# SyncE issues every transfer: the weights, their gradients and the late cache loads move from GpSimd's DMA queue to SyncE's

## The chip, the core and the metric

The kernel runs on one core of a Trainium2 chip. The core has five engines that work side by side, each with an instruction queue of its own: TensorE (PE in the profile, PEld for its weight loads), VectorE (DVE), ScalarE (ACT), GpSimd (POOL) and SyncE (SP). Sixteen DMA engines move data between the chip's memory (HBM) and the core's SBUF; a transfer is issued by an engine's queue and then runs by itself. SyncE computes nothing: it waits and issues. A transfer that SyncE issues and one that GpSimd issues go through different rings of the same sixteen DMA engines; in the profile they are q1 (hardware_dynamic) and q0 (software_dynamic).

The metric is the device time of one execution in microseconds.

## What is computed

The program is the forward and the backward pass of one decode step: a grouped-query attention block over a cache, in parallel with a bilinear gated MLP, both on the same normalised input of 2 rows of 576.

```python
x  = A_x                                  # [2, 1, 576]
xn = layernorm(x)
q = (xn @ wq) -> 32 heads of 128          # wq [576, 4096]
scores = q @ k^T * 128**-0.5              # k_cache, v_cache [2, 16, 4096, 128], 2 query heads to one of the cache
p = softmax(scores);  o = p @ v
A = o @ wo                                # wo [4096, 576]
B = ((xn @ w_gate) * (xn @ w_up)) @ w_down   # [576, 4608] twice, [4608, 576]
out_0 = x + A + B
out_1..out_8 = gradients of x, k_cache, v_cache, wq, wo, w_gate, w_up, w_down for grad_out
```

Everything is bf16. The two caches are 33.6 MB each, and their gradients as large; the five weights are 25.4 MB together, and their gradients as large. So every cache and every weight is read once and a gradient of the same size is written: by the profile 92.48 MB are read and 92.48 MB written.

## The kernel before

**Steps.** The 16 cache heads are taken two at a time (8 groups, `NG`), for each of the 2 batch rows: 16 steps, `s` in the code. A step has four cache tiles of 1 MB (K and V of two heads), each 128 partitions by 4096 elements, 8192 contiguous bytes a partition. For each tile VectorE turns 32x32 blocks (`turn`, L421), TensorE makes scores (L1105) from the turned tile, softmax and its gradient follow, TensorE contracts probabilities and their gradients with the straight tile (L1282), and the gradients of K and V are outer products (L1127) of a [4096] vector with a row of 128. For these GpSimd spreads the row into a block-diagonal tile BD (L1093, 3.6 us each, 32 of them). ScalarE and VectorE bring each product from PSUM to a 1 MB staging tile (`cp`, L425 and L427, four evictions of 128x1024 to a tile), and the tile is stored.

**Weights.** Beside the steps run 8 attention groups (wq and wo slabs of 512 columns or rows, `group_front`, `group_back`) and 9 MLP slabs of 512 (`mlp`). The gradients of the weights are outer products of short vectors as well (`rows_outer`, `cols_outer`, `tail_outer`), staged and stored in the same way. In HBM a slab of 512 columns is strided: each of its rows is a run of 1024 bytes. A 128x4x512 slab has four such runs to a partition; the 576 rows of a weight leave a tail of 64 rows of 512 columns, moved by itself. The wq tail is 128 rows of 512 bytes (L1009), as its two halves go to two halves of the partitions. A 128x4x576 slab has four runs of 1152 bytes a partition; the w_down slab has 4608 contiguous bytes.

**Buffers.** Sixteen 1 MB buffers (`big`) serve three uses with a cap each (`CAP`): straight cache tiles (8), turned tiles (13), staging tiles of stores (5). One buffer pair holds the gate and up slab (`gu`, one slot), five hold the other weight slabs (`ww`).

**Order.** No engine's order is written out by hand. The functions are generators, one for each stream of work; they yield requests (an operation on an engine with its cost, a buffer, an event, a DMA), and a planner (`Order`) runs through them in a made-up time when the program is built: of the requests that can start within a small slack of the earliest, it takes the one with the lowest priority number, and writes the instruction. Priorities are `STEP * s + PR[name]` with amendments for the first two and the last two steps (`HEAD`, `TAIL`). `Lines` is the planner's model of the two DMA rings. What engine evicts a product (ACT or DVE) is also the planner's choice (`EV`). On the chip each engine then runs its list strictly in order: an instruction that waits for a semaphore holds back everything behind it on its engine.

**Who issues.** SyncE issues the cache loads (`load_kv`, L995, in the last two steps GpSimd does), the cache gradients' stores (`put`, L654, with `KVSTORE`), w_down (L1035), and group 0's wq tail. GpSimd issues the wq, wo, gate and up slabs and tails (L1009, L1013, L1018, L1028, L1031) and all weight gradients' stores (`put` again, L654). SyncE has 132 transfers, GpSimd 136. GpSimd also builds BD (L1093) and the score weights W (L1070). ScalarE issues the two loads of x and grad_out. The transfers of a ring use eight completion semaphores in turn, so an issue waits until the one eight before it in that ring has landed.

Of the kernel before, what the change touches and what calls it, by code (L numbers as in the profile page):

```python
# [52 lines left out]
class Lines:  # L53
# [5 lines left out]
    def run(self, until=None):  # L59
        line = self.line  # L60
        while (line[0] or line[1]) and (until is None or self.now < until):
# [21 lines left out]
            for k in live:  # L83
                if line[k][0].work < 1e-9 or k == first:
                    line[k].pop(0).t = self.now + 1.4
# [19 lines left out]
class Order:  # L105
# [3 lines left out]
    def __init__(self):  # L109
# [7 lines left out]
        self.log = []  # L117

# [44 lines left out]
    def start(self, s):  # L163
        r = s.req
# [19 lines left out]
        if r[0] == "dma":  # L184
            return max(s.ready, self.free[r[1]]), r[1]
# [7 lines left out]
    def run(self):  # L193
        while self.streams:
# [37 lines left out]
            elif r[0] == "dma":  # L232
                self.free[e] = t + r[2]
                s.land = self.lines.push(e == "POOL", t + r[2] + LATENCY[e], r[3], r[4])
                s.ready = t + r[2]
                self.log.append((t, r[2], e, s.gen.__name__))
# [51 lines left out]
def DMA(engine, cost, nbytes, row=8192):  # L288
    packet = 0.0375 * row + 9.0
    return ("dma", engine, cost, 0.08 + nbytes / 16e3 * packet / row, packet)  # L290
# [4 lines left out]
CAP = {"kv": 8, "X": 13, "st": 5}  # L295
MLP0, MLPD = 0, 7.51
KVSTORE = "SP"
WQ0, WO0 = 0, 1
LATENCY, DRY = {"SP": 0.5, "ACT": 0.5, "POOL": 0.57}, 0.4
LM = 0.0  # L300
CLK = 2.0
BIAS = 0.52
SLACK = {"PE": 0.07, "ACT": 0.09, "DVE": 0.43, "POOL": 8.93, "SP": 17.19}
STEP = 28.0
HEAD = {"turn0": -27.5, "turn1": 17.9, "att": -70.5, "dsc": 20.0, "con": 10.4, "out1": 26.9, "out0": -42.2, "front": 26.2, "back": -304.6, "W0": 9.7, "W1": 90.3, "BD1": 30.3, "BD0": 91.5}
TAIL = {"turn0": 70.2, "turn1": -109.5, "att": -6.3, "dsc": -1.8, "con": -89.5, "conv": -4.6, "out1": -9.2, "out0": -5.8, "front": 37.9, "back": 9.6, "W1": -49.5, "BD1": 7.5, "BD0": -113.0, "load": -33.0}
PR = {"turn0": -74.6, "turn1": -110.6, "att": -719.4, "dsc": -725.3, "conv": 70.0, "con": -246.1, "out1": 1310.1, "out0": 250.5,
      "front": 190.0, "back": -43.0, "W0": 65.6, "W1": 62.0, "BD1": 442.2, "BD0": -91.5, "mlp": -115.0, "wout": -277.2,
      "store": 413.8, "load": -5.8, "wload": -723.6, "fin": 24.5, "const": 23.5, "mload": -44.2}


def pr(name, s):
    edge = {} if type(s) is not int else HEAD if s < 2 else TAIL if s > 13 else {}
    return STEP * s + PR[name] + edge.get(name, 0)
# [3 lines left out]
def kernel(  # L318
# [331 lines left out]
    def put(engine, parts, tag, slot, events=(), row=8192):  # L650
        def run():
            for j, (dst, src, nbytes) in enumerate(parts):
                yield DMA(engine, 0.78 if engine == "POOL" else 0.36, nbytes, row)
                (nc.gpsimd if engine == "POOL" else nc.sync).dma_start(dst, src)  # L654
# [40 lines left out]
    def rows_outer(lhs, dst, p, events=()):  # L695
# [3 lines left out]
        store = Store(FC, put("POOL", [(dst, src, 128 * FC * D * 2)], "st", i, events, 4608), p)  # L699
# [3 lines left out]
    def cols_outer(rhs, dst, p, events=()):  # L703
# [3 lines left out]
        store = Store(2, put("POOL", [(dst, src, 128 * 4 * FS * 2)], "st", i, events, 4096), p)  # L707
# [3 lines left out]
    def tail_outer(rhss, dsts, p, events=()):  # L711
# [4 lines left out]
        store = Store(2, put("POOL", parts, "tl", i, events, 4096), p)  # L716
# [20 lines left out]
    def mlp(i, Lgu, Ld, gs_slot, wd_slot):  # L737
# [42 lines left out]
        po = pr("mlp", (MLP0 + i * MLPD) / 4) + PR["wout"]  # L780
# [204 lines left out]
    def load_kv():  # L985
        n = 0
        for s in range(NS):
            g, b = divmod(s, Bq)
            yield PRIO(pr("load", s))
            for t in range(2):  # L990
                for l in range(G):
                    i = yield ACQ("kv")
                    late = s > NS - 3
                    yield DMA("POOL" if late else "SP", 0.78 if late else 0.36, 1 << 20)
                    (nc.gpsimd if late else nc.sync).dma_start(kv_t[i][:], views[t][b, G * g + l])  # L995
# [5 lines left out]
    def load_w(item):  # L1001
        kind, i = item
        if kind in ("wq", "wo"):
# [3 lines left out]
            if kind == "wq":  # L1007
                yield DMA("POOL" if i else "SP", 0.6, 128 * 256 * 2, 4096 if i else 512)
                (nc.gpsimd if i else nc.sync).dma_start(ww_t[w][:, 4 * FS:WB],  # L1009
                                                        A_wq[512:576, n0:n0 + FS].rearrange("p (h n) -> h p n", h=2))  # L1010
                yield ("lset", st["Lq"])
                yield DMA("POOL", 0.78, 128 * 4 * FS * 2, 4096)
                nc.gpsimd.dma_start(ww_t[w][:, 0:4 * FS].rearrange("p (c n) -> p c n", n=FS),  # L1013
# [424 lines left out]
```

## Time and profile before

| | us |
|---|---|
| median of 3 runs | 482.54 (481.98 to 483.42) |
| the profiled execution | 483.63 |
| its span, first to last instruction | 481.8 |
| busy PE / DVE / ACT / POOL | 377.4 / 350.0 / 345.7 / 248.6 |
| DMA: 185.93 MB in 33444 packets | mean 386 GB/s |
| mean granted TensorE clock | 0.651 |

The span is shorter than the execution by what lies before the first and after the last instruction. The page's DMA row gives the busy share of the sixteen DMA engines in 40 slices, the GB/s row what they moved; part 3 splits both by ring. A DMA engine counts as busy from a packet's start to its end, however slowly the packet moves, so a share near one and a low GB/s figure can stand together. The table by stretches gives for each engine the busy time with the number of instructions, then the granted clock, the DMA share and the GB/s. The waits name an instruction, what it waited for, the total, the number of waits and the longest.

### The profile page before, as it was taken

The page shows a single profiled execution, that of the slowest core. Times are in us where ns is not written, and L with a number is a line of the kernel's source. Part 1 is how long each engine was busy: PE and PEld are TensorE (multiplying, and loading weights), DVE is VectorE, ACT ScalarE, POOL GpSimd, SP SyncE. Part 2 cuts the span into 40 slices and gives each one's busy share as a digit, 9 for nine tenths or more (in the row PEclk, how much of TensorE's full clock was granted, in tenths as well). Part 3 has the DMA queues.
Part 4 walks back from the last instruction along what each step waited for, and adds up shares of the span by engine and source line. Part 5 has one row for each costly group of instructions (what it writes and reads, how often), then busy time and mean ns, then how long its engine had stood idle before and what let it go on. Part 6 is the DMA issues. An engine that isn't in the chain of part 4 may idle for free.

```text
span 481.8 us, 14584 instructions
## 1 busy us (share of the span) xinstructions
PE 377.4 (78%) x6122; PEld 213.5 (44%) x6122; DVE 350.0 (73%) x658; ACT 345.7 (72%) x529; POOL 248.6 (52%) x356
## 2 busy tenths in 40 slices
PE   0577977688852889879988997787797887599987
PEld 0444545443521554525553554444452545344544
DVE  6678856786747868677677878687686779398873
ACT  6059975598961688966758974799786973497993
POOL 6176803784146763451557624865715873265502
PEclk9999575666955666655555656667675665655695
DMA  8999999999999989999999999999999999999795
GB/s 298 387 402 327 414 396 422 384 379 388 423 414 373 389 335 333 400 419 398 415 399 409 366 394 422 397 413 421 411 392 421 420 416 395 402 403 375 280 407 198
DMA packets 33444, 185.93 MB, mean 386 GB/s; under 512 B 5034, under 2 KB 5170, under 8 KB 16994
## 3 DMA queue, kind: packets, MB, share of 16 engines
q1 hardware_dynamic: 18714, 131.22, 67.7%
q0 software_dynamic: 14656, 53.77, 29.7%
q8 instruction: 48, 0.79, 0.6%
q14 instruction: 18, 0.15, 0.1%
q10 hardware_dynamic: 8, 0.00, 0.0%
HBM read 92.48 MB, written 92.48 MB: 384 GB/s over the span
## 4 chain that ended last, share of the span: by engine, by line
DMA 37%; PE 29%; ACT 14%; DVE 10%; issue 5%; POOL 4%; SPq 0%; DVEq 0%; ACTq 0%; POOLq 0%
DMA out_dram<-big 23%; ACT big L425 11%; DMA gu<-in_B_w_up_dram 10%; PE ps_o L1127 6%; PE ps_m L1105 5%; PE ps_m L1282 5%; DVE big L421 4%; DMA gu<-in_B_w_gate_dram 3%; DMA big<-in_A_k_cache_dram 2%; POOL BD L1093 2%; DVE big L427 2%; PE ps_m L768 2%; PE ps_o L674 1%; PE ps_m L750 1%; PE ps_m L1193 1%
## 5 line engine op out<-in xcount | busy, mean ns | idle before, releaser
L425 ACT CAST big<-ps_o 128x1024 bf16<-128x1024 f32 (+1 forms) x324 | 288.2, 961 | 41.7 <-PE ps_o L1127 31.3
L421 DVE STREAM_TRANSPOSE big<-big 128x1024 f32<-128x1024 f32 x128 | 152.7, 1218 | 15.3 <-DMA out_dram<-big 10.8
L1093 POOL TENSOR_TENSOR BD<-vr,mask 128x2048 bf16<-128x2048 bf16 x32 | 115.3, 3602 | 31.2 <-ACT vr L425 16.6
L1105 PE MATMUL ps_m<-big,W 128*32 128x128 bf16 x2048 | 60.3, 285 | 9.6 <-POOL W L1070 4.8
L427 DVE CAST big<-ps_o 128x1024 bf16<-128x1024 f32 (+1 forms) x52 | 59.4, 1143 | 9.8 <-PE ps_o L1127 3.6
L1127 PE MATMUL ps_o<-BD,pp 32*128 32x512 bf16 x256 | 54.6, 544 | 14.1 <-ACT big L425 6.7
L1105 PEld LDWEIGHTS <-W 128*32 128x32 bf16 x2048 | 47.8, 127 | 28.4 <-issue 20.2
L654 POOL DMA_DIRECT2D out_dram<-big x43 | 33.4, 777 | 44.1 <-ACT big L425 26.5
L1070 POOL COPY W<-rep 32x16 bf16<-32x16 bf16 x128 | 24.5, 192 | 58.7 <-DVE rep L873 53.8
L1127 PE MATMUL ps_o<-BD,dd 32*128 32x512 bf16 x256 | 49.9, 530 | 6.0 <-ACT big L425 5.3
L421 DVE STREAM_TRANSPOSE big<-ww 128x1152 f32<-128x1152 f32 x25 | 34.0, 1359 | 7.6 <-DMA out_dram<-big 7.2
L1282 PE MATMUL ps_m<-big,pp 128*32 128x512 bf16 x256 | 32.1, 605 | 2.5 <-DVE accx L834 1.5
L1127 PEld LDWEIGHTS <-pp 32*128 32x128 bf16 x256 | 12.0, 99 | 37.3 <-issue 32.6
L625 POOL COPY wt<-wm 64x128 bf16<-64x128 bf16 (+1 forms) x34 | 8.9, 262 | 37.5 <-DVE wm L618 33.3
L1282 PE MATMUL ps_m<-big,dd 128*32 128x512 bf16 x256 | 26.7, 505 | 1.3 <-DVE hb L755 0.8
L421 DVE STREAM_TRANSPOSE big<-gu 128x1024 f32<-128x1024 f32 x18 | 21.8, 1223 | 3.0 <-DMA out_dram<-big 2.2
L1127 PEld LDWEIGHTS <-dd 32*128 32x128 bf16 x256 | 11.0, 99 | 26.6 <-issue 20.5
L654 POOL DMA_DIRECT2D out_dram<-tl x26 | 14.4, 557 | 15.9 <-ACT tl L425 6.6
L632 PE MATMUL ps_m<-big,wm 128*32 128x128 bf16 x416 | 13.8, 293 | 9.1 <-DVE big L421 7.9
L1292 ACT ACTIVATE osb<-ps_m 128x512 bf16<-128x512 f32 x15 | 9.1, 606 | 15.7 <-PE ps_m L1282 15.7
L674 PEld LDWEIGHTS <-xnr 32*128 32x128 bf16 x416 | 15.2, 117 | 8.3 <-issue 6.9
L674 PE MATMUL ps_o<-hb,xnr 32*128 32x128 bf16 x288 | 17.0, 271 | 2.3 <-ACT big L425 0.7
(210 smaller groups left out, 561.4 us busy)
## 6 DMA issues: line engine op xcount, KB each, us to landing
out_dram<-big SPq DMA_DIRECT2D x64, 1024.0 KB, 11.3
big<-in_A_k_cache_dram SPq DMA_DIRECT2D x28, 1024.0 KB, 12.7
big<-in_A_v_cache_dram SPq DMA_DIRECT2D x28, 1024.0 KB, 17.2
out_dram<-big POOLq DMA_DIRECT2D x26, 512.0 KB, 11.7
out_dram<-big POOLq DMA_DIRECT2D x17, 576.0 KB, 9.5
ww<-in_B_w_down_dram SPq DMA_DIRECT2D x9, 576.0 KB, 15.0
ww<-in_A_wo_dram POOLq DMA_DIRECT2D x8, 576.0 KB, 14.3
gu<-in_B_w_gate_dram POOLq DMA_DIRECT2D x9, 512.0 KB, 13.0
```

The lines of the kernel that those rows point to most:

```text
L421: nc.vector.transpose(out, in_)
L425: nc.scalar.copy(out, in_)
L427: nc.vector.tensor_copy(out=out, in_=in_)
L632: nc.tensor.matmul(dp[32 * q:32 * q + 32, 0:P], lhsT=view(Wm[:], 0, P, 8 * pos(q, s), [[1, 32]]), rhs=view(X, 0, P, xoff(q, s), [[xstep, 4 ...
L654: (nc.gpsimd if engine == "POOL" else nc.sync).dma_start(dst, src)
L674: nc.tensor.matmul(o[:, aa, dc * P:(dc + 1) * P], lhsT=xnr[32 * a:32 * a + 32, dc * P:(dc + 1) * P], rhs=rhs(a), start=True, stop=True)
L768: nc.tensor.matmul(dh, lhsT=Wdy[:, e, 2 * k:2 * k + P], rhs=view(X[:], 0, P, 64 * k + e, [[D, FC], [2, 32]]), start=(k == 0 and e == 0), s ...
L1070: nc.gpsimd.tensor_copy(view(W_t[t][w][:], 32 * a, 32, 6 + 8 * a, [[G * WW, 4], [WW, G], [1, 2]]), view(rep_t[grp[g]["qs"]][:], 32 * a, 32 ...
L1093: nc.gpsimd.tensor_tensor(BD_t[i][:], view(vr_t[v][:], 0, P, 0, [[0, 16], [1, Dh]]), view(mask16[:], 0, P, 0, [[1, 16], [0, Dh]]), ALU.mult)
L1105: nc.tensor.matmul(sc[32 * cq:32 * cq + 32, :], lhsT=view(W[:], 0, P, (be * G + l) * WW + 6 - 4 * c2 - 2 * l, [[1, 32]]), rhs=view(X[:], 0 ...
L1127: nc.tensor.matmul(o[:, k, :], lhsT=pr2[32 * c4:32 * c4 + 32, :], rhs=BD[32 * c4:32 * c4 + 32, 8 * l + 4 * h2:8 * l + 4 * h2 + 4, :], star ...
L1282: nc.tensor.matmul(ct[32 * j:32 * j + 32, :], lhsT=view(rT, 0, P, 4 * c + 2 * l, [[1, 32]]), rhs=kv_t[kvS[s][t][l]][:, Dh * c:Dh * (c + 4) ...
```

## The change

All transfers go through SyncE, except the two first loads on ScalarE, which stay. `put` always issues on `nc.sync`; `load_kv` and `load_w` as well. The wq tail becomes two transfers of 64 rows of 512 bytes, one to each half of the partitions. GpSimd keeps its compute and loses all 136 issues.

The planner is given other numbers, and all engines' orders come out anew: the priorities (`PR`, `HEAD`, `TAIL`), a new table of amendments for single steps (`OFF`), lists of the moments at which the weight slabs' loads may start (`MLP_AT`, `WQ_AT`, `WO_AT` instead of even spacing), the cap on staging buffers (4 instead of 5), the slack on GpSimd (0.47 instead of 8.93), and the model of the rings (packet costs, and the limit of eight transfers under way).

```diff
     def put(engine, parts, tag, slot, events=(), row=8192):
         def run():
             for j, (dst, src, nbytes) in enumerate(parts):
-                yield DMA(engine, 0.78 if engine == "POOL" else 0.36, nbytes, row)
-                (nc.gpsimd if engine == "POOL" else nc.sync).dma_start(dst, src)
+                yield DMA(engine, 0.36, nbytes, row)
+                nc.sync.dma_start(dst, src)
...
-        store = Store(FC, put("POOL", [(dst, src, 128 * FC * D * 2)], "st", i, events, 4608), p)
+        store = Store(FC, put("SP", [(dst, src, 128 * FC * D * 2)], "st", i, events, 4608), p)
...
-                    late = s > NS - 3
-                    yield DMA("POOL" if late else "SP", 0.78 if late else 0.36, 1 << 20)
-                    (nc.gpsimd if late else nc.sync).dma_start(kv_t[i][:], views[t][b, G * g + l])
+                    yield DMA("SP", 0.36, 1 << 20)
+                    nc.sync.dma_start(kv_t[i][:], views[t][b, G * g + l])
...
             if kind == "wq":
-                yield DMA("POOL" if i else "SP", 0.6, 128 * 256 * 2, 4096 if i else 512)
-                (nc.gpsimd if i else nc.sync).dma_start(ww_t[w][:, 4 * FS:WB],
-                                                        A_wq[512:576, n0:n0 + FS].rearrange("p (h n) -> h p n", h=2))
+                for h in range(2):
+                    yield DMA("SP", 0.36, 64 * 256 * 2, 512)
+                    nc.sync.dma_start(ww_t[w][64 * h:64 * h + 64, 4 * FS:WB],
+                                      A_wq[512:576, n0 + 256 * h:n0 + 256 * h + 256])
...
             for w, Wsrc in enumerate((B_w_gate, B_w_up)):
-                yield DMA("POOL", 0.78, 128 * 4 * FS * 2, 4096)
-                nc.gpsimd.dma_start(gu[:, 4 * w * FS:4 * (w + 1) * FS].rearrange("p (c n) -> p c n", n=FS),
+                yield DMA("SP", 0.4, 128 * 4 * FS * 2, 4096)
+                nc.sync.dma_start(gu[:, 4 * w * FS:4 * (w + 1) * FS].rearrange("p (c n) -> p c n", n=FS),
...
         if r[0] == "dma":
-            return max(s.ready, self.free[r[1]]), r[1]
+            lanes = self.lanes["SW" if r[1] == "POOL" else "HW"]
+            return max([s.ready, self.free[r[1]]] + [when(x) for x in lanes[-8:-7]]), r[1]
...
-CAP = {"kv": 8, "X": 13, "st": 5}
-MLP0, MLPD = 0, 7.51
-KVSTORE = "SP"
-WQ0, WO0 = 0, 1
+CAP = {"kv": 8, "X": 13, "st": 4}
+OFF = {"mload": {2: 138.2, 8: 8.9}, "wload": {10: 3.1, 13: 2.1}, "BD1": {1: -144.5}, "out1": {4: 2.3, 6: -20.1,
...
+MLP_AT = [0.93, 10.84, 15.91, 23.71, 30.89, 34.72, 45.87, 53.36, 60.85]
+WQ_AT = [-1, 8, 16, 24, 32, 40, 48, 56]
+WO_AT = [3, 7, 16, 26, 34, 40, 50, 58]
...
-SLACK = {"PE": 0.07, "ACT": 0.09, "DVE": 0.43, "POOL": 8.93, "SP": 17.19}
+SLACK = {"PE": 0.1, "ACT": 0.11, "DVE": 0.43, "POOL": 0.47, "SP": 17.19}
...
 def pr(name, s):
     edge = {} if type(s) is not int else HEAD if s < 2 else TAIL if s > 13 else {}
-    return STEP * s + PR[name] + edge.get(name, 0)
+    return STEP * s + PR[name] + edge.get(name, 0) + OFF.get(name, {}).get(int(s), 0)
```

In the changed program SyncE's list has 275 transfers. It begins with group 0's wq tail and slab and then the first cache tiles; the last cache load is followed by 12 stores of 1 MB, 3 of 576 KB, 4 of 512 KB and small ones. Line numbers of the changed kernel are 9 to 11 higher than those above (L425 becomes L436, L654 becomes L665, L995 becomes L1005).

## The prediction

> **What bounds the kernel now.** I read the page first (the engines' shares, then the DMA lines), then the busy time by stretches, the DMA view of single stretches, and last the waits of SyncE's queue.
>
> The page and its two queues:
>
> ```profile
> PE 377.4 (78%) x6122; PEld 213.5 (44%) x6122; DVE 350.0 (73%) x658; ACT 345.7 (72%) x529; POOL 248.6 (52%) x356
> DMA  8999999999999989999999999999999999999795
> DMA packets 33444, 185.93 MB, mean 386 GB/s; under 512 B 5034, under 2 KB 5170, under 8 KB 16994
> q1 hardware_dynamic: 18714, 131.22, 67.7%
> q0 software_dynamic: 14656, 53.77, 29.7%
> ```
>
> No engine is over 80% busy; the 16 DMA engines are busy nearly throughout. So the transfers bound it, and the question is how fast the bytes go. q1 is SyncE's ring, q0 GpSimd's.
>
> By stretches (the last column is GB/s, the one before it the DMA share):
>
> ```profile
> 36.00:44.00 8.00, 5.80 (x117) 3.25 (x117) 7.29 (x14) 8.00 (x13) 6.04 (x5) 1.00 0.85 281
> 72.00:84.00 12.00, 9.15 (x167) 6.49 (x167) 7.58 (x19) 6.85 (x14) 4.01 (x13) 0.57 1.01 423
> 120.00:132.00 12.00, 10.77 (x236) 7.39 (x239) 9.06 (x23) 11.38 (x20) 1.23 (x5) 0.97 1.01 423
> 176.00:192.00 16.00, 14.97 (x248) 7.26 (x241) 13.49 (x23) 11.84 (x16) 8.10 (x20) 0.58 0.96 325
> 192.00:264.00 72.00, 63.06 (x960) 34.13 (x958) 49.09 (x90) 52.91 (x86) 35.64 (x56) 0.53 1.02 406
> 442.00:458.00 16.00, 15.06 (x230) 8.66 (x227) 14.68 (x25) 14.64 (x23) 10.15 (x9) 0.61 0.74 281
> ```
>
> A full DMA share can mean 423 GB/s or 325. The DMA view says which ring ran: from 120 to 132 us
>
> ```profile
> DMA packets 696, 5.08 MB, mean 423 GB/s; under 512 B 77, under 2 KB 77, under 8 KB 77
> q1 hardware_dynamic: 694, 5.05, 100.5%
> ```
>
> from 182 to 186 us
>
> ```profile
> DMA packets 348, 1.17 MB, mean 292 GB/s; under 512 B 69, under 2 KB 69, under 8 KB 346
> q0 software_dynamic: 340, 1.15, 98.7%
> ```
>
> and from 40 to 42 us, behind the first wq tail (L1009) that GpSimd issues:
>
> ```profile
> DMA packets 155, 0.25 MB, mean 126 GB/s; under 512 B 104, under 2 KB 104, under 8 KB 145
> q0 software_dynamic: 138, 0.17, 58.8%
> ```
>
> SyncE's ring alone moves 423 GB/s, GpSimd's alone 292 here and 356 from 418 to 424 us, the two mixed about 406. 185.93 MB at 423 are 439.6 us; the span is 481.8. The 42 us between are what can be won: by stretches about 3.4 in the first 8 us (a mean of 246 GB/s), 2.7 from 36 to 44, 3.7 from 176 to 192, 5.4 from 442 to 458, 7 after 458, the rest a few per cent everywhere.
>
> SyncE's queue is mostly waiting:
>
> ```profile
> SPq L654 <- ACT big L425: 155.8, 42, 14.4
> SPq L654 <- DVE big L427: 91.9, 17, 14.9
> SPq L995 <- DMA out_dram<-big: 32.8, 8, 18.7
> ```
>
> Its stores wait for evictions (L425, L427); its loads for a staging buffer whose store has to land.
>
> **The change, part by part.** All 136 GpSimd transfers join the 132 of SyncE; with the wq tails split in two, the changed program has 275 there.
>
> *Issue.* SyncE's issue takes 0.33 to 0.34 us where it doesn't wait; 143 more are 48 us, in a queue that waits over 300: nothing on the path. If SyncE never waited, 275 x 0.34 = 94 us would still fit five times. GpSimd loses 95 us of issuing (43 stores at 777 ns, 26 tails at 557, the loads at 544 to 870) of its 248.6; what waits behind these are the BD products (L1093, 3.6 us) and the copies of W. The chain of waits shows few of them. Zero; bounds -5 to 0.
>
> *The seven wq tails* (L1009). Each, on GpSimd, leaves 112 packets of 32 bytes in the packet records, and the bytes lost against 423 GB/s around the seven are 2.4, 0.9, 1.0, 0.6, 1.6, 0.3 and 0.3 us, 7.1 in all. From SyncE group 0's tail went as 128 packets of 512 bytes at 27 ns: 128 x 27 / 16 = 0.2 us. But around 40 us ACT is busy 8.00 of 8.00 us with evictions that SyncE's first stores wait for, and that stays. I take -5, bounds -7 to 0.
>
> *GpSimd's ring alone.* In the packet records SyncE's ring is all but empty in 32 of the 482 stretches of 1 us while GpSimd's runs; without those counted above and those of the tail, 20 us at about 330 GB/s. At 405 (4096 bytes in 161 ns, 16 engines) they are 16.3: -4, and -1 for packets that trail into the next stretch. -5, bounds -6 to 0.
>
> *The mixed stretches.* 44:72, 84:120, 192:264, 276:372 and 396:442 lose 12.6 us together. Some 4 are the price of smaller packets (25.4 bytes a ns at 4096, 26.5 at 8192) and stay. Of the 8 others I give over half to the second ring: -5, bounds -8 to 0. Against these two terms speaks that the 292 and the 423 GB/s, at DMA shares near one, carried different things: strided runs of 1 KB there, rows of 8192 bytes here. If that and not the ring made the difference, both terms are zero (rival A).
>
> *Packet size.* No SyncE row shows a strided slab (128 x 4 runs of 1024 or 1152 bytes). On GpSimd they went as packets of 4096 (7472) and 4608 bytes (3200). SyncE's nearest rows, the 512-byte tail and the 1152-byte rows of x, made one packet of each run (27 and 49.5 ns). If the slabs do so, a 1024-byte run is 45 ns by interpolation, four are 180 instead of 161: 7472 x 19 / 16 = 8.9 us, and 4 x 49.5 = 198 instead of 181 gives 3.4 more. Bounds 0 to +12.3. These rows speak for the upper end; that packets overlap a little (DMA shares of 1.02) speaks against it. +5.
>
> *One line instead of two.* Every issue waits for the landing of the one eight before it, until now in each ring by itself, and a store that waits for an eviction holds every load behind it. With 1 MB transfers eight are 8.4 MB, 20 us of work at 423, longer than any wait above. Around an mlp group (512, 64, 512, 64, 576 KB, then 1 MB, then two 32 KB halves) eight are 2.9 MB or 7 us, shorter than the longest waits. Bounds 0 to +25 (the 32 us that the second ring covered, at 330 GB/s, would be 10.5 MB or 25 us to make up). The order puts loads of small pieces together, and outstanding stores are capped at 4 buffers instead of 5. I take +1, near the lower end: SyncE's long waits stand where 8 MB are in flight.
>
> *Start.* The wq slab is first in line instead of landing at 13.0 us from GpSimd; q follows sooner, but loads fill the lines until 36 us either way. -1, bounds -3 to 0.
>
> *The tail.* After the last cache load landed (441 us) the old order had 11.7 MB to store, 28 us at 423, and took 40.8: ACT, busy 12.00 of 12.00 us from 456 to 468, could not feed the lines. In the new order 16.8 MB (12 stores of 1 MB, 3 of 576 KB, 4 of 512 KB, small ones) stand behind the last load, so the loads come earlier and the lines have more to do beside the last evictions. About as many evictions follow the last transpose (22 against 21). -4, bounds -8 to 0.
>
> Sum: -5 - 5 - 5 + 5 + 1 - 1 - 4 = -14, a span of 467.8 us. The profiled execution took 483.63, 1.8 more than its span, and 1.1 more than the median of 482.54; on the median's scale 468.5 us.
>
> **Rivals.**
>
> *A. The bytes matter, not the ring.* Both ring terms are zero, the sum is -4: 478.5 us. For it: 372 to 396 us runs at 419 GB/s with GpSimd's ring at a third of the packets' time. Against it: that ring alone also carried 8192-byte cache rows from 418 to 424 us, at 356. The Trainium skill has this as a rule: "DMA: Bandwidth & Descriptors", section "Issuing engines are not separate DMA queues", says that transfers of all issuing engines end on the same 16 DMA engines and interleave, so that who issues saves issue time alone. By that rule the time is this rival's, and the two rows at 356 and 423 are where this trace differs from it.
>
> *B. One line blocks (slower).* SyncE's queue holds loads behind a store that waits for ACT or DVE. Place: the mlp groups, with 7 us in flight. Price: with the 25 us and nothing won but the 7 of the wq tails, 482.5 + 25 - 7 = 500. It decides once dry time passes about 15 us, what the other terms win. For it: waits of 14 to 19 us in that queue. Against it: the lines are full during most of these.
>
> *C. Nothing measurable.* Rival A with the packet size between the +5 taken and its +12.3: 478.5 + 4 = 482.5.
>
> *D. All gains whole.* Ring rate 423 for 8192-byte rows, 405 for the others: 134.2 MB and 50.7 MB take 317 + 125, code 2, start 3, the final output 4, a dry tail of 5: 456.
>
> **How the numbers follow.** The forecast's surroundings, 460 to 475, hold 0.53; D 0.12; A 0.14; C 0.05; B 0.16. The predicted time is the first's, 468.5. The range reaches down to D (455) and up over A and C into half of B (486). Three tenths of a per cent, 1.4 us, is what a measurement of this kernel tells from no change. Faster: 0.53 + 0.12 + 0.14 = 0.79, and 0.01 of B, where little dries up: 0.80. Same 0.05, slower 0.15. For the forecast's case alone: 460 to 475.
>
> **What the profile after would show.** Right: q0 gone, q1 over 95%, stretches of 5 us and more at 415 to 423 GB/s in the middle, no 32-byte packets, mean over 395 GB/s. Packet size shows in the count: about 34,000 packets if slabs stay whole, 66,000 if each run is a packet. B would show DMA shares under 0.8 in the middle, with SyncE waiting for evictions just before. A would show DMA shares near one at 390 GB/s as now. The tail would show over 400 GB/s behind the last load. What would make it wrong: strided slabs that run at 290 GB/s on SyncE's ring as well, since 51 MB at that rate are 50 us more than at 405; no row excludes this, and I count it in B.

## The result

The change makes the kernel a little slower: a median of 485.04 us (482.73 to 486.81, 20 runs) against 482.03 (479.70 to 486.41, 20 runs) for the kernel before, a ratio of 1.0054, with an interval of 1.0033 to 1.0074. That is 3.0 us by the ratio of the medians, 2.6 by the ratio given. The forecast was 468.5 and faster.

The page of the changed kernel: the engines, the DMA share in 40 slices, the packets, the one ring that is left.

```profile
span 482.8 us, 14538 instructions
PE 367.1 (76%) x6122; PEld 209.5 (43%) x6122; DVE 352.8 (73%) x667; ACT 345.9 (72%) x520; POOL 155.5 (32%) x220
...
DMA  7999999999999999999999999999999999999985
...
DMA packets 65266, 185.90 MB, mean 385 GB/s; under 512 B 4393, under 2 KB 47665, under 8 KB 48817
...
q1 hardware_dynamic: 65192, 184.96, 99.2%
```

GpSimd lost 93 us of busy time (248.6 to 155.5), one ring carries everything, and the packet count doubled from 33444 to 65266, as it does if every run of 1024 or 1152 bytes becomes a packet. But the mean rate went from 386 GB/s to 385, where the forecast wanted over 395.

The stretches of the changed kernel, with the columns of the table in the prediction (busy time of PE, PEld, DVE, ACT and POOL, the granted clock, the DMA share, GB/s):

```profile
0.00:8.00 8.00, 0.00 (x0) 0.00 (x0) 6.89 (x34) 5.42 (x10) 3.82 (x18) 1.00 0.61 228
8.00:440.00 432.00, 333.04 (x5696) 190.75 (x5696) 320.27 (x583) 311.19 (x468) 143.40 (x196) 0.68 1.02 393
440.00:483.00 43.00, 34.05 (x426) 18.79 (x426) 25.64 (x51) 29.33 (x43) 8.25 (x6) 0.55 0.84 330
84.00:96.00 12.00, 9.75 (x185) 5.39 (x188) 11.03 (x18) 10.98 (x14) 7.01 (x11) 0.78 0.94 307
...
176.00:192.00 16.00, 14.23 (x253) 7.10 (x246) 13.61 (x23) 13.03 (x19) 5.54 (x10) 0.73 1.03 413
192.00:264.00 72.00, 55.71 (x950) 32.01 (x938) 49.86 (x95) 54.50 (x84) 24.52 (x36) 0.69 1.03 396
442.00:458.00 16.00, 14.86 (x202) 8.97 (x200) 11.83 (x24) 14.52 (x24) 6.64 (x4) 0.50 1.03 410
```

The same two long stretches of the kernel before:

```profile
8.00:440.00 432.00, 341.65 (x5623) 193.35 (x5623) 315.86 (x568) 307.29 (x475) 227.45 (x322) 0.64 1.01 397
440.00:482.00 42.00, 35.72 (x507) 20.15 (x499) 28.26 (x57) 32.36 (x46) 13.78 (x14) 0.66 0.76 298
```

The tail is better, 330 GB/s instead of 298: the 14.2 MB it moves would have taken 47.6 us at the old rate and took 43. The start is a little worse (228 GB/s against 245). The long middle is 1% worse, at a DMA share of 1.02: 4 GB/s over 432 us are 1.7 MB, or 4.4 us. The gain of the tail is given back there, with the DMA engines busy nearly all the time. The two profiled executions differ by 1.0 us and the medians by 3.0, so the stretches hold only a part of the difference.

The stretch from 176 to 192 us, slow before at 325 GB/s, now has 413; others have become slow. The DMA view of the changed kernel from 88 to 96 us, with loads and stores around an mlp group:

```profile
DMA packets 1405, 2.16 MB, mean 270 GB/s; under 512 B 91, under 2 KB 1248, under 8 KB 1338
...
q1 hardware_dynamic: 1403, 2.13, 88.4%
```

1248 of 1405 packets are under 2 KB. By the packet records 1.19 of the 2.16 MB are runs of 1 KB, the rest is w_down and rows of 8192 bytes. The stretch moves 270 GB/s at a queue share of 0.88, which would be 306 for a full one: where most bytes are strided, SyncE's ring is about as slow as the 292 that was laid to GpSimd's.

SyncE's waits for evictions are shorter than before:

```profile
SPq L665 <- ACT big L436: 88.7, 53, 7.4
SPq L665 <- DVE big L438: 19.5, 11, 5.7
```

The stores' waits for evictions fell from 155.8 and 91.9 us to 88.7 and 19.5. That is not the new order's doing alone: the old order with every transfer on SyncE (below) has 75.0 and 35.2.

### The profile page after: what moved, and what is told of

It is laid out like the page before. It is cut to its first block, busy times and chain, and to the rows that moved or that the text cites. A ratio compares the mean times of both kernels' runs of the same rounds, so it can differ in the third digit from the quotient of the medians.

```text
span 482.8 us, 14538 instructions
## 1 busy us (share of the span) xinstructions
PE 367.1 (76%) x6122; PEld 209.5 (43%) x6122; DVE 352.8 (73%) x667; ACT 345.9 (72%) x520; POOL 155.5 (32%) x220
## 2 busy tenths in 40 slices
DMA packets 65266, 185.90 MB, mean 385 GB/s; under 512 B 4393, under 2 KB 47665, under 8 KB 48817
## 4 chain that ended last, share of the span: by engine, by line
DMA 58%; PE 17%; ACT 9%; DVE 8%; issue 4%; SPq 3%; DVEq 0%; ACTq 0%
DMA out_dram<-big 26%; DMA gu<-in_B_w_up_dram 12%; DMA gu<-in_B_w_gate_dram 9%; ACT big L436 8%; DMA ww<-in_A_wo_dram 7%; DVE big L432 5%; PE ps_o L1138 4%; DMA big<-in_A_v_cache_dram 3%; PE ps_m L1293 2%; PE ps_m L1116 2%; PE ps_m L779 2%; DMA ww<-in_B_w_down_dram 2%; SPq L1042 2%; DVE big L438 1%; PE ps_m L900 1%
## 5 line engine op out<-in xcount | busy, mean ns | idle before, releaser
L436 ACT CAST big<-ps_o 128x1024 bf16<-128x1024 f32 (+1 forms) x325 | 289.9, 961 | 39.0 <-PE ps_o L1138 28.8
L438 DVE CAST big<-ps_o 128x1024 bf16<-128x1024 f32 (+1 forms) x51 | 56.0, 1097 | 10.2 <-PE ps_o L1138 4.1
L1116 PE MATMUL ps_m<-big,W 128*32 128x128 bf16 x2048 | 58.3, 279 | 4.5 <-POOL W L1081 1.7
L1138 PE MATMUL ps_o<-BD,pp 32*128 32x512 bf16 x256 | 50.6, 549 | 9.6 <-ACT big L436 6.4
L1138 PE MATMUL ps_o<-BD,dd 32*128 32x512 bf16 x256 | 46.5, 496 | 6.2 <-ACT big L436 5.3
L761 PE MATMUL ps_m<-gu,xs 128*32 128x128 bf16 x360 | 11.1, 279 | 26.7 <-DMA gu<-in_B_w_gate_dram 17.3
L1293 PE MATMUL ps_m<-big,dd 128*32 128x512 bf16 x256 | 23.9, 457 | 1.0 <-DVE hb L785 0.7
L764 ACT COPY gs<-ps_m 128x256 f32<-128x256 f32 x9 | 3.5, 384 | 29.2 <-PE ps_m L761 29.2
L761 PEld LDWEIGHTS <-xs 128*32 128x32 bf16 x360 | 7.7, 121 | 30.9 <-DMA gu<-in_B_w_gate_dram 19.4
L766 DVE TENSOR_TENSOR hb<-gs,ps_m 128x128 bf16<-128x128 f32 x9 | 2.6, 285 | 19.8 <-ACT gs L764 19.8
```

What stands on the lines that cost most here:

```text
L436: nc.scalar.copy(out, in_)
L438: nc.vector.tensor_copy(out=out, in_=in_)
L761: nc.tensor.matmul(ug[32 * a:32 * a + 32, 1 - w, :], lhsT=xs[:, dc if dc < 4 else 4 + w, :], rhs=gu[:, FS * k + P * a:FS * k + P * (a + 1) ...
L1116: nc.tensor.matmul(sc[32 * cq:32 * cq + 32, :], lhsT=view(W[:], 0, P, (be * G + l) * WW + 6 - 4 * c2 - 2 * l, [[1, 32]]), rhs=view(X[:], 0 ...
L1138: nc.tensor.matmul(o[:, k, :], lhsT=pr2[32 * c4:32 * c4 + 32, :], rhs=BD[32 * c4:32 * c4 + 32, 8 * l + 4 * h2:8 * l + 4 * h2 + 4, :], star ...
L1293: nc.tensor.matmul(ct[32 * j:32 * j + 32, :], lhsT=view(rT, 0, P, 4 * c + 2 * l, [[1, 32]]), rhs=kv_t[kvS[s][t][l]][:, Dh * c:Dh * (c + 4) ...
```

## The experiments

Four groups: which half of the change acts, what the bytes cost by their pattern in HBM, what each kind of transfer costs by itself, and whether single terms of the sum can be had alone. The ratios are each against the kernel before, run beside it on the same chip; the two kernels without computation ran once each. "Idle" below is the time in which the sixteen DMA engines together were short of full busyness, worked out from the packet records.

**New order, two rings.** The changed kernel, its order kept, with the strided slabs, the weights' tails and the weight gradients issued by GpSimd.

```diff
-                nc.sync.dma_start(dst, src)
+                (nc.sync if row == 8192 else nc.gpsimd).dma_start(dst, src)
```

and `nc.gpsimd` for the loads of wq, wo, gate and up.

> The changed kernel with its new order kept on every engine, but the strided weight slabs and tails (wq, wo, gate, up) and all weight gradients issued by GpSimd again; cache transfers, w_down and the wq tails stay with SyncE. Theory P (on SyncE's ring every contiguous run is a packet, 1024 bytes in 46 ns, and this costs some 13 us of the DMA engines): packets fall from 65266 to about 34000, their time in all from 483 to about 470 us, and the kernel is faster than the changed one: 470 to 478 us. Theory O (the new order, or one line, is what costs): with the order kept it stays at 483 to 487 us, whatever the packets.

**Old order, one ring.** The kernel before, its order kept, with every transfer on SyncE.

```diff
-                (nc.gpsimd if engine == "POOL" else nc.sync).dma_start(dst, src)
+                nc.sync.dma_start(dst, src)
```

and `nc.sync` in `load_kv` and `load_w`; the wq tail stays one transfer.

> The kernel before with its old order kept, but every transfer issued by SyncE. Theory P: the packets' time rises by 13 us as in the changed kernel, the wq tails' stalls (7 us) go, and an order made for two lines leaves gaps: 487 to 500 us, slower than the changed kernel. Theory O: at or under the kernel before, 475 to 483 us, as only the ring differs.

Measured: 489.58 us, a ratio of 1.0175 (1.0119 to 1.0230), and 491.98, 1.0206 (1.0167 to 1.0244). With the two kernels of the study this fills a table (medians, us):

| | two rings | one ring |
|---|---|---|
| old order | 482.0 | 492.0 |
| new order | 489.6 | 485.0 |

Each order is best with the rings it had. In the first run the packets were few again and their time in all fell by 10 us, from 483 to 472, as Theory P wanted; the kernel was slower than the changed one all the same, with about 23 us of idle time instead of 14.4. In the old order one line (all transfers in one queue) costs 10 us, and the new order, which does nothing good for two rings, makes up 7 of them. So "SyncE issues every transfer" is a loss that the new order mostly repairs. By stretches, the old order on one ring:

```profile
8.00:440.00 432.00, 325.62 (x5508) 187.62 (x5508) 309.25 (x557) 298.57 (x465) 139.50 (x195) 0.67 1.01 387
440.00:490.00 50.00, 41.68 (x626) 22.78 (x614) 35.03 (x69) 39.56 (x56) 11.85 (x7) 0.70 0.85 331
```

Again the DMA share stays at 1.01 in the middle while the rate falls by 10 GB/s; 10 of 397 over 432 us are 11 us, more than the 8.7 us by which the span grew. The tail gives some of it back, at 331 GB/s. Between 40 and 440 us the DMA engines are no more idle than in the kernel before (3.5 against 3.4 us), so this loss is not one of lines that run dry.

**Contiguous slabs, in both kernels.** The weights are read, and their gradients written, as if each slab lay in HBM as one block with 4096 or 4608 contiguous bytes a partition. Same bytes, same instructions; the weights then lie permuted, so the result is another one and only the time is of use.

```diff
+def flat(t, i):
+    return bass.AP(t.tensor, t.offset + i * 262144, [[2048, 128], [1, 2048]])
...
-                                    A_wq[0:512, n0:n0 + FS].rearrange("(c p) n -> p c n", p=P))
+                                    flat(A_wq, i))
```

and likewise for gate, up and the three gradients; in wo, out_5 and out_8 the partition becomes the outer index.

> The changed kernel with the same number of transfers, bytes and the same order, but the 512-column slabs read and written as 4096 contiguous bytes a partition and the 576-wide ones as 4608, so that weights and weight gradients lie permuted in HBM (another computation, for its time only). Theory P: about 35700 packets, packet time down by 18 to 22 us, 463 to 470 us. Theory O: 483 to 487 us as now. Theory H (the 1 KB runs are slow at HBM itself, on either ring): as P here, but then the next run wins as much.

> The kernel before with the same edit: slabs contiguous in HBM, GpSimd's ring as it was. Theory P: packets stay at 33444 (GpSimd's ring already packs four runs in one packet), so little is won: 477 to 482 us. Theory H: 463 to 472 us.

Measured: 478.77 (0.9926, 0.9899 to 0.9953) for the changed kernel, 476.53 (0.9883, 0.9831 to 0.9935) for the one before. Against their own strided versions they gain 1.3% or 6 us and 1.2% or 5.5 us. So the scattered runs of 1 KB cost about 6 us whichever ring carries them; that is Theory H's pattern at well under half of its size. And the new kernel stays 2 us behind the old one although its packets are now few:

```profile
DMA packets 35697, 185.90 MB, mean 390 GB/s; under 512 B 4392, under 2 KB 8240, under 8 KB 19248
```

Its middle is still 4 GB/s behind that of the old kernel with the same edit. First the new one:

```profile
8.00:440.00 432.00, 338.21 (x5726) 193.67 (x5727) 324.64 (x590) 314.60 (x475) 143.27 (x196) 0.68 1.00 399
```

and the old one:

```profile
8.00:440.00 432.00, 351.47 (x5750) 199.28 (x5751) 324.13 (x584) 315.81 (x486) 215.72 (x321) 0.65 1.00 403
```

By the medians, then, the split into 65,000 packets is a small part of the difference between the two kernels, and what is left is order and line. The intervals (about 3 us on the difference of the two gains) do not exclude that the split costs the whole 3 us.

**What transfers cost alone.** A kernel without any computation: the same kinds of transfers, 13 to 17 MB of each, one kind after the other, from SyncE or from GpSimd.

> No computation: one kind of transfer after another, each alone, with a wait for all between: 16 cache tiles of 1 MB in on SyncE; 26 strided slabs of 512 KB in on SyncE, then on GpSimd; the same bytes contiguous on SyncE, then on GpSimd; then the same five as stores; 1 MB stores on GpSimd; strided stores on GpSimd beside cache loads on SyncE; both mixed on SyncE; eight wq tails on GpSimd, eight on SyncE. Theory P: strided slabs on SyncE at 350 to 360 GB/s, on GpSimd at 400; contiguous on either at 405. Theory H (runs of 1 KB are slow at HBM on either ring): strided at 350 to 380 on both, contiguous over 400 on both. The prediction's ring terms would need GpSimd's ring alone under 380 GB/s with 8192-byte rows too.

Measured, by stretches (DVE and POOL busy, clock, DMA share, GB/s). The kinds are, in order: 1 MB tiles in, SyncE; strided slabs in, SyncE and GpSimd; contiguous slabs in, SyncE and GpSimd; tiles out, SyncE; strided out, SyncE and GpSimd; contiguous out, SyncE and GpSimd; tiles out, GpSimd; tiles with strided slabs on two rings, then on SyncE's alone; eight wq tails from GpSimd; the same from SyncE, each as one transfer.

```profile
2.00:42.00 40.00, 0.00 (x0) 0.00 (x0) 1.00 1.00 417
46.00:84.00 38.00, 0.61 (x13) 0.00 (x0) 1.00 1.09 348
91.00:129.00 38.00, 0.61 (x13) 16.90 (x23) 1.00 1.02 341
134.00:167.00 33.00, 0.61 (x13) 0.00 (x0) 1.00 1.02 407
172.00:205.00 33.00, 0.61 (x13) 11.90 (x23) 1.00 1.02 409
209.00:248.00 39.00, 0.00 (x0) 0.00 (x0) 1.00 1.01 419
252.00:291.00 39.00, 0.61 (x13) 0.00 (x0) 1.00 1.04 340
296.00:337.00 41.00, 0.64 (x13) 17.45 (x24) 1.00 0.98 321
341.00:374.00 33.00, 0.60 (x13) 0.00 (x0) 1.00 1.02 405
378.00:412.00 34.00, 0.61 (x13) 12.38 (x24) 1.00 1.01 389
417.00:458.00 41.00, 0.00 (x0) 7.24 (x14) 1.00 1.00 406
462.00:536.00 74.00, 0.61 (x13) 17.58 (x24) 1.00 1.01 409
539.00:615.00 76.00, 0.71 (x13) 0.00 (x0) 1.00 1.04 397
619.00:627.00 8.00, 0.00 (x0) 4.59 (x6) 1.00 0.29 67
631.00:642.00 11.00, 0.00 (x0) 0.00 (x0) 1.00 0.14 42
```

SyncE's ring is the faster one by 2% for strided slabs in, 3% for tiles out, 4% for contiguous slabs out and 6% for strided slabs out, and 0.5% the slower for contiguous slabs in. The pattern makes the large difference: 348 GB/s for scattered runs of 1 KB against 407 for the same bytes in one block. In a mix with tiles the scattered runs are nearly hidden (409 and 397). Why the split into packets costs nothing here can be read from the packet records: a GpSimd packet of four scattered runs took 194 ns on average, and four SyncE packets at 51 ns each take 203 and overlap more (a DMA share of 1.09 against 1.02). The same 4096 bytes in one block took 163 ns on either ring.

The rule of the Trainium skill that rival A drew on ("DMA: Bandwidth & Descriptors", "Issuing engines are not separate DMA queues") says that who issues changes the issue time alone. These rows agree with it to within 6%.

**How slabs and tiles take turns.** No computation again: tiles and strided slabs in alternating groups, on two rings, or on SyncE's in groups of 2 slabs and 3 tiles, 4 and 6, 8 and 12; then small transfers.

> No computation: 39 cache tiles in beside 26 strided slabs out, four times: slabs on GpSimd and tiles on SyncE; all on SyncE with two slabs to three tiles; four to six; eight to twelve; then gate and up slabs with their tails in, on SyncE alone and on GpSimd alone; tail rows out on either; wq tails in halves on SyncE. Theory I (slabs run at 330 GB/s alone on either ring and hide among cache rows; a second ring mixes them packet by packet, one ring only as its order does): 405 to 415 GB/s with two rings, 400 to 410 at two to three, falling to 375 to 390 at eight to twelve. Theory R (rings do not matter at all): the four within 1%.

The four mixed stretches:

```profile
45.00:176.00 131.00, 0.88 (x18) 18.36 (x25) 1.00 1.01 417
178.00:310.00 132.00, 0.93 (x18) 0.00 (x0) 1.00 1.02 407
312.00:442.00 130.00, 0.92 (x18) 0.00 (x0) 1.00 1.03 414
444.00:575.00 131.00, 0.98 (x18) 0.00 (x0) 1.00 1.03 407
```

Two rings 417, one ring 407 to 414, whatever the grouping; the fall to 375 that Theory I wanted did not come. So one ring costs 1 to 2.5% in such a mix, and how finely the kinds alternate within it doesn't matter here. With one execution, and 1.7% between the three groupings on one ring, that is not much more than the scatter. By the packet records the two rings do mix the kinds: none of their 131 stretches of 1 us has over 70% of its bytes from slabs, while the three groupings on one ring have 25, 30 and 28 such stretches. The small transfers, SyncE first: a gate slab, its tail, an up slab and its tail run at 318 GB/s from SyncE and 294 from GpSimd; a row of tails of weight gradients, 64 KB each, goes out in 0.64 us each from SyncE and 0.52 from GpSimd.

**Alternating in the real order.** The packet records say that in the changed kernel slabs run by themselves more often: 90 of the stretches of 1 us have over 70% of their bytes from slabs (w_down's counted with them), against 45 before. So the planner was told to alternate: after a slab take a tile, after a tile a slab, if one can start within 0.5 us, or, in the second run, within SyncE's whole slack of 17 us.

```diff
+                near = [c for c in cand if c[3] == e and c[0] <= t + SLACK[e]]
+                if e == "SP":
+                    other = [c for c in near if (c[2].req[4] < 300) != self.slab and c[0] <= t + 0.5]
+                    near = other or near
...
+                if e == "SP":
+                    self.slab = s.req[4] < 300
```

> The changed kernel with one more rule for SyncE's line when the order is made: of the transfers that can start within 0.5 us of the first, one of the other kind (slab or cache tile) than the last goes first. Runs of slabs in the line: 55 of one slab instead of 8, 10 of four or more instead of 17. Theory I: fewer stretches of slabs alone, more GB/s in the middle, 476 to 482 us. Theory O (the order found is good as it is, and any other is worse): 486 us and more.

> The same rule among all transfers within the planner's whole slack of 17 us. Theory I: as the last run or better, 474 to 482 us. Theory O: worse than it, as loads wait behind stores that are not ready, 488 us and more.

Measured: 500.73 (1.0362, 1.0329 to 1.0394) and 501.05 (1.0385, 1.0351 to 1.0419). Slower than the changed kernel by 16 us. SyncE's waits for evictions on ACT rose from 88.7 us to

```profile
SPq L672 <- ACT big L443: 118.5, 54, 10.5
```

and the DMA engines, idle for 14.4 us of the span in the changed kernel, are so for 29.9. That is nearly all of the 16 us. The largest piece lies from 218 to 236 us, at a DMA share of 0.61, while SyncE's stores wait 11.7 us for ACT. Of the stretches with over 70% slab bytes none went away: 91 instead of 90. The order that the planner made was a worse one, and it did not even mix better on the rings. So this doesn't decide whether better mixing would help.

**Parts of the move, in the new order.** The weight gradients' stores alone back on GpSimd, the strided loads alone (as in the first run), and 44 tails alone: 18 of gate and up, 26 of the gradients.

```diff
 # the stores
-                nc.sync.dma_start(dst, src)
+                (nc.sync if row == 8192 else nc.gpsimd).dma_start(dst, src)
 # the tails of a weight gradient; those of gate and up go to nc.gpsimd in load_w
+                (nc.gpsimd if tag == "tl" else nc.sync).dma_start(dst, src)
```

> The changed kernel, order kept, with the weight gradients' stores alone issued by GpSimd (the loads stay with SyncE). Issuing all slabs from GpSimd took 489.6 us against 485.0. Theory F (the new order fits one line, and a second ring lets stores run ahead of the loads that they were planned behind): most of those 4.6 us come from the stores, 487 to 490 us. Theory G (it is GpSimd's late issue of loads, behind its compute): 483 to 486 us.

> The changed kernel, order kept, with the strided weight loads alone issued by GpSimd (wq and wo slabs, gate and up with their tails). Theory F: 483 to 486 us. Theory G: 487 to 490 us, with the mlp's first product waiting for its slabs.

> The changed kernel, order kept, with only the 64-row tails (18 gate and up tails in, 26 gradient tails out) issued by GpSimd. Theory L with the tails as the small pieces that hurt: w_down's packets back from 223 to 185 ns, 480 to 484 us. If it is the slabs and not the tails, or GpSimd's waiting in place: 485 to 488 us.

Measured: 487.75 (1.0133, 1.0102 to 1.0165), 487.34 (1.0116, 1.0093 to 1.0139) and 483.76 (1.0022, 0.9995 to 1.0049). Either half on the second ring is worse by 3 to 4 us than the one ring for which the order was found, so neither Theory F nor G has it alone. With the tails on GpSimd the kernel is 1.5 us faster than the changed one by the ratios, with an interval of about as much, so it can hardly be told from none; w_down's packets fell from 223 ns to 204, half of what Theory L wanted.

**Parts of the move, in the old order.** The weights' loads alone on SyncE, the weight gradients' stores alone, the late cache loads alone.

```diff
 # the loads, in load_w: wq, wo, gate, up and their tails
-                nc.gpsimd.dma_start(...)
+                nc.sync.dma_start(...)
 # the stores, in put
-                (nc.gpsimd if engine == "POOL" else nc.sync).dma_start(dst, src)
+                nc.sync.dma_start(dst, src)
 # the late cache loads
-                    (nc.gpsimd if late else nc.sync).dma_start(kv_t[i][:], views[t][b, G * g + l])
+                    nc.sync.dma_start(kv_t[i][:], views[t][b, G * g + l])
```

The first and the third also have the wq tails on SyncE, in halves.

> The kernel before, order kept, with the weight loads alone (wq, wo, gate, up and tails; the wq tails in halves) issued by SyncE; stores and late cache loads as before. Theory L (loads of many small pieces in SyncE's line run alone at about 310 GB/s and hold the cache loads back): 487 to 491 us, most of the 10 us. Theory S (a store in the line that waits for its eviction holds the loads behind it): 481 to 485 us.

> The kernel before, order kept, with the weight gradients' stores alone issued by SyncE. Theory S: 487 to 491 us, with more idle time of the DMA engines. Theory L: 481 to 485 us.

> The kernel before, order kept, with the eight cache loads of the last two steps issued by SyncE, and the wq tails in halves from SyncE (which alone took 482.2 us). Both theories of a cost in the line: these eight are full 1 MB rows and need nothing of ACT, so 480 to 484 us. If the late loads are a cost of their own (they stand in SyncE's line behind stores that wait for evictions, in the stretch where ACT is the busiest engine): 485 to 489 us.

Measured: 499.26 (1.0318, 1.0278 to 1.0357), 490.67 (1.0157, 1.0102 to 1.0212) and 483.14 (0.9987, 0.9962 to 1.0012). The late cache loads are free. The stores alone cost 8 us, the loads alone 15: more than both together (10), and more than either theory allowed. In the run with the loads the middle loses 7 GB/s, 3.0 MB or 8 us of the 16; the rest is lost behind 440 us:

```profile
8.00:440.00 432.00, 323.64 (x5428) 183.77 (x5429) 303.57 (x550) 297.16 (x462) 186.23 (x264) 0.67 1.00 390
440.00:498.00 58.00, 46.23 (x694) 24.06 (x693) 40.76 (x75) 41.84 (x58) 17.41 (x15) 0.68 0.68 268
```

58 us at a DMA share of 0.68: the work that the middle didn't do is left for a tail that can't fill the ring. The DMA engines are idle for 19 us there, against 10 before. SyncE's longest wait there is that of a store for VectorE's eviction (the waits from 440 to 498 us):

```profile
SPq L654 <- DVE big L427: 30.3, 6, 15.8
```

In the run with the stores on SyncE, the DMA engines are idle for 10.1 us between 40 and 440 us, against 3.4 before. Nearly all that was added lies from 392 to 416 us, at a DMA share of 0.73: SyncE issues nothing but stores from 396 to 419 us, and they wait for ACT and VectorE. Here are the waits from 392 to 416 us, first this run, then the kernel before:

```profile
SPq L654 <- ACT big L425: 17.8, 3, 12.2
SPq L654 <- DVE big L427: 9.4, 3, 5.4
```

```profile
SPq L654 <- DVE big L427: 29.5, 3, 14.6
SPq L654 <- ACT big L425: 3.3, 2, 2.3
```

The stores waited there before as well, and longer; but then GpSimd's ring went on beside them, and the rate was 404 GB/s or more from 372 to 442 us.

**The wq tails alone.** The kernel before with the seven tails of L1009 on SyncE, as one transfer each, and as two halves (the edit of the second):

```diff
-                (nc.gpsimd if i else nc.sync).dma_start(ww_t[w][:, 4 * FS:WB],
-                                                        A_wq[512:576, n0:n0 + FS].rearrange("p (h n) -> h p n", h=2))
+                for h in range(2):
+                    nc.sync.dma_start(ww_t[w][64 * h:64 * h + 64, 4 * FS:WB],
+                                      A_wq[512:576, n0 + 256 * h:n0 + 256 * h + 256])
```

> The kernel before, order kept, with the seven wq tails issued by SyncE instead of GpSimd. Theory W (the prediction's step: these tails stall the DMA engines and lose 7.1 us): no 32-byte packets, 475 to 479 us. Theory N (the stalls lie where eviction or HBM hold the lines up, and the tails only stand there): 481 to 484 us.

> The kernel before, order kept, with the seven wq tails issued by SyncE as two transfers of 64 rows each, as the changed kernel does. As one transfer of two halves they took SyncE's ring 1.6 us each when nothing else ran, and the kernel 484.1 us. Theory W2 (a tail's own time is what counts, and halved it is short): 476 to 481 us. Theory N (the tails are not what holds the lines up where they stand): 481 to 484 us.

Measured: 484.11 (1.0054, 1.0032 to 1.0075) as one transfer, 482.21 (0.9993, 0.9972 to 1.0015) in halves. The hole did fill: in the second kernel the stretch that had 281 GB/s reads

```profile
36.00:44.00 8.00, 5.76 (x126) 3.34 (x123) 7.34 (x14) 7.71 (x13) 3.60 (x1) 0.96 1.02 403
8.00:440.00 432.00, 334.73 (x5623) 189.39 (x5624) 316.33 (x568) 307.09 (x475) 221.46 (x315) 0.66 1.00 396
```

but the whole middle has 396 GB/s, where it had 397. The microseconds won at 40 us were lost again later: from 396 to 442 us the rate is 376 GB/s, where it was 404, and from 396 to 410 us SyncE's stores wait 10.1 us for ACT and 5.8 for VectorE. As one transfer a tail takes 1.6 us alone on SyncE against 1.0 on GpSimd, and 0.62 for each half. The Trainium skill ("DMA: Bandwidth & Descriptors", "Why a DMA increments its semaphore by 16 and not by 1") says that a transfer is spread over the largest number of engines up to 16 that divides the outermost dimension of both sides. For this tail as one transfer that is 2, as its two halves are the outermost dimension in HBM. The measured 1.6 us agrees: 64 packets of 512 bytes an engine at 27 ns are 1.7 us.

## Why the prediction was wrong

The direction was wrong: two terms of -5 rested on a cause that isn't there, a third was won and lost again, and a fourth was mis-sized. By its steps:

*Issue* (0): not contradicted. GpSimd is freed of 93 us in the old order on one ring too, and that kernel is 10 us slower; no run has this term by itself.

*The seven wq tails* (-5): failed. Filling the hole at 36 to 44 us moves the end by 0 (0.9993, 0.9972 to 1.0015). The step took bytes lost in one stretch as time lost at the end; in that run they were lost again from 396 to 442 us, behind stores that wait for evictions. The cost of a tail on SyncE was wrong as well: 128 x 27 / 16 = 0.2 us takes all sixteen engines for granted, but alone the tail takes 1.6 us as one transfer and 1.24 in two halves.

*GpSimd's ring alone* (-5) and *the mixed stretches* (-5): failed, and these make the sign. The price run shows 348 against 341 and 419 against 406 GB/s by ring, 348 against 407 by pattern, and a mix that is faster, not slower, on two rings (409 against 397, 417 against 407 to 414). The slow stretch at 292 GB/s was strided slabs by themselves (all but 0.02 of its 1.17 MB by the packet records). On SyncE's ring, where the forecast had such bytes at 405 GB/s, they ran at 345; and the stretches of 1 us in which slabs and tiles mix (20 to 70% of the bytes from slabs) ran at 390 in the changed kernel, where before they ran at 399. The two contiguous kernels gain 6 and 5.5 us on one ring and on two. The prediction had this in hand: it noted that the 292 and the 423 GB/s carried different things, and gave it 0.14 as rival A. The row that it held against A, 356 GB/s with cache rows on GpSimd's ring from 418 to 424 us, did not bear the weight: 0.84 of its 2.14 MB were packets of strided slabs, and alone, tiles go out at 406 on that ring (tiles in were not priced there). The 292 itself is lower than any price (321 to 348), and that stays unexplained.

*Packet size* (+5, bounds 0 to 12.3): the split came exactly as the 512 and 1152-byte rows said, a packet for each run, at 48.9 ns for 1024 bytes. Its price was too high if anything: alone it is nil (348 against 341 GB/s), and with the split taken out of both kernels the difference between them is 2.2 us instead of 2.6 to 3.0. The step compared four packets of a run each, 180 ns, with 161 ns for GpSimd's packet. That 161 is the median in the trace before, where most slabs run beside tiles (the mean is 176); of slabs alone a packet takes 194. A price up to the whole 3 us is not excluded.

*One line instead of two* (+1, bounds 0 to 25): the term that was mis-sized. In the old order one line costs 10 us, whatever the split into packets costs included. With the stores alone on SyncE it costs 8, and there it is rival B's mechanism: DMA engines that run dry, 7 us more than before, while SyncE's stores wait for ACT and VectorE. With everything on SyncE it is not: the middle has no more idle time than before, and the 10 us come at full DMA engines. In the new order 7 of the 10 are made up. That the long waits "stand where 8 MB are in flight" was true and not enough: the rate falls without idle time. What goes with it is that slabs follow slabs (90 stretches of 1 us with over 70% of slab bytes, 45 before) instead of running beside tiles; between 8 and 440 us there are some 75 of them at 345 GB/s, where before there were 32 at 351 and the mixed ones ran at 399. For the old order on one ring the whole count is 88. In the price run one ring likewise has 25 to 30 such stretches where two have none, at a cost of 1 to 2.5%. That this grouping is the cause in the kernel was not shown: the run that should have broken it up made no difference to the count.

*Start* (-1): wrong in sign and small; 245 to 228 GB/s over 8 us is 0.3 us lost.

*The tail* (-4): right in size. 410 GB/s from 442 to 458 us instead of 281, and idle time behind 440 us fell from 10.1 to 7.3 us; at the old rate its bytes would have taken 4.6 us more. But the old order on one ring has 331 GB/s there as well, with more bytes left over by its slower middle, so part of this gain is work put off and not won.

With 0 for the rings and the tails of wq, +4.4 for the middle, +0.3 for the start and -4.6 for the tail the stretches give about 0; the spans differ by 1.0, the medians by 3.0. Of the 4.4, packets and line can't be parted closer than above. Nor were the parts of the new order (priorities, start times of the loads, 4 staging buffers instead of 5) tried one by one.

The signs named beforehand were good ones: DMA shares near one at 390 GB/s are what rival A was to show (385 came), and the 65,266 packets what the split was to show. What would make it wrong was named too, strided slabs as slow on SyncE's ring; it was 345 GB/s and not 290, and it was counted in B. Rival A's own time, 478.5, did not come, as it kept the one line at +1. The share under 0.8 that B was to show didn't come in the changed kernel; there the loss on one line takes the form of full DMA engines at a lower rate.

The steps that failed are thus the two ring terms, which gave GpSimd's ring the blame for the pattern of its bytes, and the wq tails; that the change comes out slower goes with one line in place of two, priced at 1: 10 us in the old order, of which the new one makes up 7. Why one line costs 10 us at full DMA engines stays open. So do why the alternating orders run dry, why the loads alone on SyncE cost more than loads and stores together, and why slab stretches run at 345 GB/s inside the kernel and at 385 to 388 in the mixed price run.

## What to carry to other kernels

When a stretch of a trace is slow at a full DMA share, price its bytes by pattern and ring apart, in a small kernel with transfers alone, before putting the blame on the ring that happened to carry them. A hole filled in the middle of an order that is fixed beforehand is not time won at the end. And an order found for one set of queues is worth testing only with those queues: here each of the two orders loses 5 to 10 us on the other's queues.

## What the hardware showed that was not expected

- Scattered runs of 1 KB (rows 8 or 9 KB apart in HBM) move at 340 to 348 GB/s from SyncE, contiguous slabs at 405 to 407. Beside 1 MB tiles the loss is nearly hidden: 397 to 417 for the mix. Inside the kernel the loss was 1.2 to 1.3% of its time.
- SyncE's ring makes one packet of each such run (42,240 for the slabs and 64-row tails of the changed kernel, where GpSimd's made 10,560 of four runs each) and is no slower for it alone: four packets of 51 ns against one of 194, which in one contiguous block takes 163.
- A 64 KB store of 64 rows costs 0.52 us when GpSimd issues a row of them and 0.64 from SyncE, 127 and 102 GB/s. A 64 KB load whose outermost dimension is 2 costs 1.6 us from SyncE, and two loads of 32 KB in its place 0.62 each.
- Two rings in a mix were a little faster than one, in one execution each: 417 against 407 to 414, and 409 against 397.
